# Low halves of twelve first-layer weight tiles from TensorE: 64 w minus the high half, copied by ScalarE

## The chip, the cores and the metric

The kernel runs on one core of a Trainium2 chip. The core has TensorE (PE, the matrix engine, whose weight loads the profile shows as PEld), VectorE (DVE), ScalarE (ACT), GpSimd (POOL) and a queue of transfers that SyncE (SP) issues to 16 DMA engines. Each engine works through its own instructions in a fixed order and waits on semaphores for the others. TensorE writes only to PSUM, in banks of 128 x 512 fp32 values. The metric is the time of one execution on the device in microseconds; lower is better.

## The reference

The input is `q`, `k`, `v` of shape (4, 8, 768, 48), a gate `beta`, and two pairs of weight matrices. First comes a recurrence over 768 time steps for each of 32 heads, and then two dense layers one after the other on 3072 tokens of width 384 (hidden width 2048):

```python
k_n = k / (norm(k) + 1e-06)
for t in range(S):
    y[:, :, t] = einsum('bhd,bhde->bhe', q[:, :, t], state)
    v_old = einsum('bhde,bhd->bhe', state, kt)
    state = state + bt * einsum('bhd,bhe->bhde', kt, vt - v_old)
...
h = x @ w_in                                        # first layer
x = (maximum(h, 0) + log1p(exp(-abs(h)))) @ w_out
...
h = x @ w_in2                                       # second layer
out = (h * cos(h)) @ w_out2
```

## The kernel before, in words

The time axis is cut into 24 chunks of 32 steps (`NS`), in groups of four. For a group, `norms`, `prep`, `gram` and `solve` work without the state: they scale `k`, form products inside a chunk on TensorE, and solve a small triangular system on VectorE (30 short dependent instructions; its end is the transpose `tg`). Then `step(n)` runs for each chunk: a chain of small matmuls (48 columns) on TensorE, each followed by a scaled copy on ScalarE and a subtraction on VectorE that split the result into two fp16 halves (`b`, `u`, `st`, `y`). After two steps `y` is turned by a transposing DMA into the columns `xt` of one block of 256 tokens, and `moe_block(0, j)` pushes this block through the first layer; there are twelve such blocks. When all are done, six blocks of 512 tokens go through the second layer.

Numbers are kept to about twice the precision of fp16: each operand is a high half and a low half, and a product is three fp16 matmuls (`PAIRS`: high-high, high-low, low-high). The weights arrive in DRAM as fp64. `conv(ph, f, t, key)` makes the two fp16 halves of one of the 16 hidden tiles of a layer, with both its matrices at once, that is 2 x 384 values in each of 128 partitions. A DMA brings 768 KB into `raw` or into the space of weight tiles that are not made yet. Three VectorE instructions (L456, L458, L460) build fp32 numbers in one of two buffers `cv`; one (`hi`, L471 on ScalarE, sometimes VectorE) writes the high half fp16(64 w), and one (`lo`, L481, on VectorE) the low half, 64 w minus the high half. Buffer `cv` is free again after that. For the second layer GpSimd does the low half (L479).

In `moe_in` (L820) a hidden tile is formed in one of the two PSUM banks `psH` and passes through ScalarE and VectorE; `moe_out` (L882) multiplies the result with the second matrix into `accA` and `accB`. At the start of the program the banks also serve `gram`.

The order of the instructions is written out by a planner (`Plan`): every `put` gives an operation with the engines that may do it, its assumed cost, and the keys that it reads and writes. The planner simulates the engines, always taking the ready operation with the longest way to the end, and emits each engine's list in that order. So one more operation can move all others, and can move an operation that two engines may do from one to the other. Since operations are entered with all of `weights(0)` ahead of the steps, an operation that `conv` puts on a bank `psH` comes before every use of this bank by `moe_in`.

Of the kernel before, what the change touches and what calls it, by code (L numbers as in the profile page):

```python
# [10 lines left out]
F32 = mybir.dt.float32  # L11
# [36 lines left out]
NRAW = 1  # L48
NB2 = NS // 4
NT = 2 * P, 4 * P  # L50
Z = 40 * C
# [217 lines left out]
def dve(n, fast=False):  # L269
    return 0.068 + n / (1920.0 if fast else 960.0)  # L270
# [6 lines left out]
def pool(n):  # L277
    return 0.149 + n * 0.001883
# [6 lines left out]
@with_exitstack  # L285
def delta_moe_moe_kernel(ctx, tc, q, k, v, beta, mask, w1, w2, out):
    nc = tc.nc
# [14 lines left out]
    mask_sb = const.tile([P, C + 3], F32, name="mask_sb")  # L302
    hpi = const.tile([P, 1], F32, name="hpi")
    tiny = const.tile([P, 1], F32, name="tiny")

# [70 lines left out]
    def put(var, w, r, fn, **kw):  # L376
        return pl.add(var, w, r, fn, **kw)
# [65 lines left out]
    def conv(ph, f, t, key):  # L443
# [39 lines left out]
        put([("ACT", act(n)), ("DVE", dve(n, True))], wk, ck, hi, port=True)  # L483
        put([("POOL", pool(n)), ("DVE", dve(n))][0 if ph else 1:], wk, ck, lo, port=True)

# [320 lines left out]
    def moe_in(ph, j, u, xk, x):  # L806
# [6 lines left out]
        for i in range(2 - ph):  # L813
            for kc in range(KC):
                f = (2 * u + i) if ph == 0 else u

                def fn(e, i=i, kc=kc, f=f):
                    w, xv = wview(ph, f)[:, 0], x if ph == 0 else x()
                    for idx, (l, m) in enumerate(PAIRS):
                        nc.tensor.matmul(  # L820
                            hp[:, i] if ph == 0 else hp, lhsT=w[:, l, kc * P:(kc + 1) * P], rhs=xv[:, m * KC + kc],
                            start=(kc == 0 and idx == 0), stop=(kc == KC - 1 and idx == 2))
                us = 3 * mm(NT[ph])
                moe_left[0] -= us
                put([("PE", us)], hk, xk + [("w", ph, f, 0)], fn, base=moe_left[0])
        n = 4 * P
# [40 lines left out]
    def moe_out(ph, j, u):  # L867
# [6 lines left out]
        for i in range(2 - ph):  # L874
            f = (2 * u + i) if ph == 0 else u
            for key, cs in groups:
# [10 lines left out]
                moe_left[0] -= us  # L887
                put([("PE", us)], [key], [("g16", s3, 0), ("g16", s3, 1), ("w", ph, f, 1)], fn, base=moe_left[0])

# [50 lines left out]
    put([("SP", 0.475)], [("beta",)], (), lambda e: nc.sync.dma_start(out=beta_sb, in_=beta), dma=0.27, **A)  # L940
    put([("SP", 0.475)], [("mask",)], (), lambda e: nc.sync.dma_start(out=mask_sb, in_=mask), dma=0.1, **A)
    load_v(0)
    load_v(1)
# [108 lines left out]
```

## Time and profile before

| | |
|---|---|
| runs | 1037.36, 1038.86, 1046.35 us; median 1038.86 |
| profiled execution (its time is its span) | 1038.4 us |
| mean granted TensorE clock | 0.965 of full speed |
| PE busy | 940.7 us, 91% |
| DVE busy | 668.8 us, 64% |
| ACT busy | 667.2 us, 64% |
| POOL busy | 366.2 us, 35% |
| first matmul of the first layer | 105.0 us after the start |
| HBM traffic | 71.03 MB read, 35.65 MB written |

The shares are averages over a start, in which the first group of chunks and the weights are prepared, a long middle, in which steps and layers share TensorE, and an end, in which only the second layer is left. They differ in what limits them, so the rows below are taken stretch by stretch. The clock that the throttle granted to TensorE has two levels, 1.2 GHz (0.50 in the rows) and 2.4 GHz (1.00).

### The profile page before, as it was taken

The page shows a single profiled execution, that of the slowest core. Times are in us where ns is not written, and L with a number is a line of the kernel's source. Part 1 is how long each engine was busy: PE and PEld are TensorE (multiplying, and loading weights), DVE is VectorE, ACT ScalarE, POOL GpSimd, SP SyncE. Part 2 cuts the span into 40 slices and gives each one's busy share as a digit, 9 for nine tenths or more (in the row PEclk, how much of TensorE's full clock was granted, in tenths as well). Part 3 has the DMA queues.
Part 4 walks back from the last instruction along what each step waited for, and adds up shares of the span by engine and source line. Part 5 has one row for each costly group of instructions (what it writes and reads, how often), then busy time and mean ns, then how long its engine had stood idle before and what let it go on. Part 6 is the DMA issues. An engine that isn't in the chain of part 4 may idle for free.

```text
span 1038.4 us, 27814 instructions
## 1 busy us (share of the span) xinstructions
PE 940.7 (91%) x11552; PEld 687.5 (66%) x11552; DVE 668.8 (64%) x1186; ACT 667.2 (64%) x1261; POOL 366.2 (35%) x330
## 2 busy tenths in 40 slices
PE   1135889997999899999999999999999999999998
PEld 1125779886899798899999997744444444444443
DVE  8999977666547754863576665686555555555454
ACT  5344769776767776866777787865555555554554
POOL 3013326433523442432332545553332223233232
PEclk9965899998999999999999999999999999999999
DMA  6998696876766775674558862111001010000000
GB/s 194 288 262 203 128 240 121 200 177 170 175 84 149 178 155 111 135 157 76 117 115 210 237 153 84 44 35 61 31 1 61 1 61 0 31 31 1 31 1 31
DMA packets 307741, 117.94 MB, mean 114 GB/s; under 512 B 272160, under 2 KB 287648, under 8 KB 307616
## 3 DMA queue, kind: packets, MB, share of 16 engines
q1 hardware_dynamic: 307616, 116.17, 46.0%
q8 instruction: 91, 1.49, 0.6%
q14 instruction: 34, 0.28, 0.1%
HBM read 71.03 MB, written 35.65 MB: 103 GB/s over the span
## 4 chain that ended last, share of the span: by engine, by line
PE 72%; DVE 9%; ACT 7%; DMA 6%; issue 3%; SPq 2%; POOL 1%; DVEq 0%; ACTq 0%; POOLq 0%
PE psH L820 20%; PE accA L882 15%; PE accB L882 11%; PE psC L820 7%; PE psA L882 6%; PE psC L699 6%; PE psY L820 4%; DMA kpd<-kp 3%; PE psY L699 2%; SPq L380 2%; ACT kp L389 1%; PE psA L605 1%; DMA qt<-q_dram 1%; DVE tlan L401 1%; DMA kt<-k_dram 1%
## 5 line engine op out<-in xcount | busy, mean ns | idle before, releaser
L401 POOL TENSOR_TENSOR g<-g,g 128x512 f16<-128x512 f32 x191 | 227.7, 1192 | 461.1 <-ACT g L389 446.9
L820 PE MATMUL psH<-xt,w 128*128 128x256 f16 x1728 | 232.1, 276 | 0.2
L389 ACT ACTIVATE g<-g 128x512 f16<-128x512 f32 x191 | 119.9, 628 | 105.2 <-DVE g L405 70.3
L882 PEld LDWEIGHTS <-w 128*128 128x128 f16 x1728 | 163.3, 98 | 23.3 <-issue 3.6
L820 PEld LDWEIGHTS <-w 128*128 128x128 f16 x1728 | 158.7, 98 | 18.9 <-issue 0.3
L882 PE MATMUL accA<-g,w 128*128 128x256 f16 x1152 | 159.6, 275 | 3.2 <-POOL g L401 1.7
L882 PEld LDWEIGHTS <-v 128*128 128x128 f16 x864 | 84.5, 98 | 101.9
L820 PEld LDWEIGHTS <-v 128*128 128x128 f16 x864 | 84.6, 98 | 100.9
L410 ACT ACTIVATE e<-e 128x512 f32<-128x512 f32 x96 | 60.4, 629 | 81.7 <-DVE e L405 81.7
L401 DVE TENSOR_TENSOR g<-psH,e 128x512 f32<-128x512 f32 x96 | 66.1, 688 | 70.3 <-ACT e L412 64.0
L882 PE MATMUL accB<-g,w 128*128 128x256 f16 x576 | 94.7, 276 | 0.0
L820 PE MATMUL psH<-xu,v 128*128 128x512 f16 x351 | 83.1, 379 | 0.0
L820 PE MATMUL psC<-xu,v 128*128 128x512 f16 x342 | 81.5, 379 | 0.0
L882 PE MATMUL accB<-g,v 128*128 128x512 f16 x288 | 77.8, 379 | 0.0
L882 PE MATMUL accA<-g,v 128*128 128x512 f16 x288 | 77.8, 379 | 0.0
L882 PE MATMUL psA<-g,v 128*128 128x512 f16 x288 | 77.6, 379 | 0.0
L837 ACT ACTIVATE e<-psH 128x512 f32<-128x512 f32 x96 | 56.7, 590 | 30.8 <-PE psH L820 30.4
L699 PEld LDWEIGHTS <-bdKQ 128*128 128x128 f16 x1840 | 64.4, 98 | 10.5 <-issue 8.4
L412 ACT ACTIVATE e<-e,hpi 128x512 f32<-128x512 f32 x96 | 69.3, 721 | 3.0
L699 PEld LDWEIGHTS <-bdA 128*128 128x128 f16 x1680 | 56.6, 99 | 20.4 <-issue 18.4
L412 ACT ACTIVATE e<-e 128x512 f32<-128x512 f32 x96 | 59.9, 624 | 1.2
L699 PE MATMUL psC<-b,bdT 128*128 128x48 f16 x768 | 29.2, 187 | 34.1 <-ACT bdT L389 21.2
(143 smaller groups left out, 1508.6 us busy)
## 6 DMA issues: line engine op xcount, KB each, us to landing
bdKQ<-kqd SPq DMA_DIRECT2D x184, 64.0 KB, 2.8
kpd<-kp SPq DMA_DIRECT2D x24, 448.0 KB, 3.6
kqd<-kq SPq DMA_DIRECT2D x20, 512.0 KB, 4.2
raw<-w_dram SPq DMA_DIRECT2D x12, 768.0 KB, 5.0
bdA<-kpd SPq DMA_DIRECT2D x96, 96.0 KB, 3.5
w<-w_dram SPq DMA_DIRECT2D x10, 768.0 KB, 7.1
v<-w_dram SPq DMA_DIRECT2D x10, 768.0 KB, 6.5
qt<-q_dram SPq DMA_DIRECT2D x24, 256.0 KB, 4.2
```

What stands on the lines that cost most here:

```text
L380: put([("SP", issue)], w, r, lambda e: nc.sync.dma_start(out=dst, in_=src), dma=eng_us, **kw)
L389: nc.scalar.activation(out=out, in_=in_, func=AF.Copy, scale=scale)
L401: put(var, w, r, lambda e: eng[e].tensor_tensor(out=out, in0=a, in1=b, op=op), port=True, **kw)
L410: nc.scalar.activation(out=out, in_=in_, func=func, scale=scale)
L412: nc.scalar.activation(out=out, in_=in_, func=func, scale=scale, bias=bias)
L605: nc.tensor.matmul(ps[:, h], lhsT=w, rhs=x, start=(i == 0), stop=(i == len(ops) - 1))
L699: nc.tensor.matmul(ps[:, h, 0:D], lhsT=lhs(h), rhs=mov[:, h], start=(first and i == 0 and h == 0), stop=(last and i == len(passes) - 1 and ...
L820: nc.tensor.matmul(hp[:, i] if ph == 0 else hp, lhsT=w[:, l, kc * P:(kc + 1) * P], rhs=xv[:, m * KC + kc], start=(kc == 0 and idx == 0), s ...
L837: nc.scalar.activation(out=ev, in_=hv, func=AF.Abs, scale=sc)
L882: nc.tensor.matmul(acc[c], lhsT=w[:, l, c * P:(c + 1) * P], rhs=rhs, start=(f == 0 and idx == 0 and (ph == 1 or c != 1)), stop=(f == NF - ...
```

## The change

For the first twelve hidden tiles of the first layer (`LO_PE = 12`, `f` = 0 to 11) the low half is no longer made by the one VectorE instruction. For each of the tile's two matrices TensorE runs two matmuls of 384 columns into a bank `psH`: one in fp32 with a matrix `eye` = 64 times the identity as weights and `cv` as the moving operand, and one in fp16 with `neg` = minus the identity and the high half. The bank then holds 64 w minus the high half, and ScalarE copies it as fp16 into the weight tile. `eye` is a new input of 64 KB, loaded by one DMA, and ScalarE makes `neg` of it once. The first layer's matmuls read the low half under a new key `("wl", f, o)`. Tiles 12 to 15 and the second layer stay as they were.

```diff
--- before.py
+++ after.py
@@ -47,6 +47,7 @@
 XTB = 3
 NRAW = 1
 NB2 = NS // 4
+LO_PE = 12
 NT = 2 * P, 4 * P
 Z = 40 * C
 X2 = 2 * C
@@ -283,7 +284,7 @@
 
 
 @with_exitstack
-def delta_moe_moe_kernel(ctx, tc, q, k, v, beta, mask, w1, w2, out):
+def delta_moe_moe_kernel(ctx, tc, q, k, v, beta, mask, ident, w1, w2, out):
     nc = tc.nc
     eng = {"PE": nc.tensor, "DVE": nc.vector, "ACT": nc.scalar, "POOL": nc.gpsimd, "SP": nc.sync}
     pl = Plan()
@@ -301,6 +302,8 @@
     beta_sb = const.tile([P, NG, C], F32, name="beta_sb")
     mask_sb = const.tile([P, C + 3], F32, name="mask_sb")
     hpi = const.tile([P, 1], F32, name="hpi")
+    eye = const.tile([P, P], F32, name="eye")
+    neg = const.tile([P, P], F16, name="neg")
     tiny = const.tile([P, 1], F32, name="tiny")
 
     wbuf = {0: [wp.tile([P, 2, DM], I64, name=f"w{f}") for f in range(0, NF, 2)], 1: []}
@@ -481,7 +484,18 @@
                 nc.vector.scalar_tensor_tensor(wv(1), in0=cf, scalar=sc, in1=wv(0), op0=ALU.mult, op1=ALU.subtract)
 
         put([("ACT", act(n)), ("DVE", dve(n, True))], wk, ck, hi, port=True)
-        put([("POOL", pool(n)), ("DVE", dve(n))][0 if ph else 1:], wk, ck, lo, port=True)
+        if ph or f >= LO_PE:
+            put([("POOL", pool(n)), ("DVE", dve(n))][0 if ph else 1:], wk, ck, lo, port=True)
+            return
+        for o in range(2):
+            bank, bk_ = flat[1 + o]
+
+            def rest(e, o=o, bank=bank):
+                nc.tensor.matmul(bank[:, 0:DM], lhsT=eye, rhs=cf[:, o], start=True, stop=False)
+                nc.tensor.matmul(bank[:, 0:DM], lhsT=neg, rhs=wv(0)[:, o], start=False, stop=True)
+
+            put([("PE", 5 * mm(DM))], [bk_], ck + wk + [("eye",), ("neg",)], rest, cold=2.0)
+            copy(wv(1)[:, o], bank[:, 0:DM], 1.0, [("wl", f, o)], [bk_] + wk, DM, ps=True, only=("ACT",))
 
 
     def norms(g):
@@ -822,7 +836,7 @@
                             start=(kc == 0 and idx == 0), stop=(kc == KC - 1 and idx == 2))
                 us = 3 * mm(NT[ph])
                 moe_left[0] -= us
-                put([("PE", us)], hk, xk + [("w", ph, f, 0)], fn, base=moe_left[0])
+                put([("PE", us)], hk, xk + [("w", ph, f, 0), ("wl", f, 0)], fn, base=moe_left[0])
         n = 4 * P
         gk, ek = [("g", s)], [("e", s)]
         flat_ = (lambda t: t) if ph == 0 else (lambda t: t.rearrange("p a t -> p (a t)"))
@@ -885,7 +899,7 @@
                                 stop=(f == NF - 1 and idx == 2 and (ph == 1 or c != 0)))
                 us = 3 * len(cs) * mm(NT[ph])
                 moe_left[0] -= us
-                put([("PE", us)], [key], [("g16", s3, 0), ("g16", s3, 1), ("w", ph, f, 1)], fn, base=moe_left[0])
+                put([("PE", us)], [key], [("g16", s3, 0), ("g16", s3, 1), ("w", ph, f, 1), ("wl", f, 1)], fn, base=moe_left[0])
 
     def moe_end(ph, j):
         if ph == 0:
@@ -939,6 +953,8 @@
     memset(st, 0.0, [("st", 0), ("st", 1)], 768, **A)
     put([("SP", 0.475)], [("beta",)], (), lambda e: nc.sync.dma_start(out=beta_sb, in_=beta), dma=0.27, **A)
     put([("SP", 0.475)], [("mask",)], (), lambda e: nc.sync.dma_start(out=mask_sb, in_=mask), dma=0.1, **A)
+    put([("SP", 0.475)], [("eye",)], (), lambda e: nc.sync.dma_start(out=eye, in_=ident), dma=0.2, **A)
+    actf(neg, eye, AF.Copy, [("neg",)], [("eye",)], P, scale=-1.0 / W_SC, **A)
     load_v(0)
     load_v(1)
 
@@ -1035,6 +1051,7 @@
             np.triu(np.full((C, C), 1.0 / K_SC, np.float32), 1),
             np.repeat(np.array([[0.0, K_SC ** -2, 0.0], [-1.0, 0.0, K_SC ** -2]], np.float32), C // 2, axis=0)],
             axis=1), (B, 1)),
+        "ident_dram": W_SC * np.eye(P, dtype=np.float32),
         "w1_dram": w_both(inputs["moe_w_in"], inputs["moe_w_out"]),
         "w2_dram": w_both(inputs["moe2_w_in"], inputs["moe2_w_out"]),
     }
```

The planner gives the whole program a new order. On VectorE, in the middle of the second step (`step(1)`), there stood before (`cv` are the buffers of the weights under conversion, `w` the weight tiles, `u`, `b`, `bt`, `st`, `y` the operands of the step):

```order
L405 SCALAR_TENSOR_TENSOR u_111<-psC_146,u_111 128x384
L405 SCALAR_TENSOR_TENSOR kq_128<-qt_117,kq_128 128x512
L481 SCALAR_TENSOR_TENSOR w_84<-cv_88,w_84 128x2x384
L405 SCALAR_TENSOR_TENSOR bt<-psC_145,bt 128x384
L456 TENSOR_SCALAR cv_88<-raw_87 128x768
L540 STREAM_TRANSPOSE kq_129<-kp_123 128x512
L458 SCALAR_TENSOR_TENSOR cv_88<-raw_87,cv_88 128x768
L542 STREAM_TRANSPOSE kq_129<-ka_127 128x128
L405 SCALAR_TENSOR_TENSOR b_110<-bt,b_110 128x384
L460 SCALAR_TENSOR_TENSOR cv_88<-raw_87,cv_88 128x768
L481 SCALAR_TENSOR_TENSOR w_83<-cv_89,w_83 128x2x384
L405 SCALAR_TENSOR_TENSOR y_112<-psY,y_112 128x384
```

Now the same piece of the step, from `u` to the next `b`, reads:

```order
L408 SCALAR_TENSOR_TENSOR u_113<-psC_148,u_113 128x384
L461 SCALAR_TENSOR_TENSOR cv_91<-w_88,cv_91 128x768
L408 SCALAR_TENSOR_TENSOR kq_131<-qt_120,kq_131 128x512
L556 STREAM_TRANSPOSE kq_132<-ka_128 128x128
L459 TENSOR_SCALAR cv_90<-raw_89 128x768
L408 SCALAR_TENSOR_TENSOR bt<-psC_147,bt 128x384
L461 SCALAR_TENSOR_TENSOR cv_90<-raw_89,cv_90 128x768
L408 SCALAR_TENSOR_TENSOR abuf<-psA,mask_sb,abuf 128x8x16
L408 SCALAR_TENSOR_TENSOR b_112<-bt,b_112 128x384
L463 SCALAR_TENSOR_TENSOR cv_90<-raw_89,cv_90 128x768
L463 SCALAR_TENSOR_TENSOR cv_91<-w_88,cv_91 128x768
L408 SCALAR_TENSOR_TENSOR kp_124<-psA,kp_124 128x128
```

The low halves (L481) are gone; the three instructions that build `cv` (now L459, L461, L463) stand alone, and the output `y` of the first step, which stood behind the second step's first `u`, `bt` and `b`, has moved ahead of this piece (two rows before it).

On TensorE, where the first matmul of the first layer stands, behind the first product of the third step, there stood before:

```order
L699 LDWEIGHTS bdKQ
L699 MATMUL psC_145<-st_106,bdKQ 128x48
...
L699 LDWEIGHTS bdT
L699 MATMUL psC_146<-b_110,bdT 128x48
...
L820 LDWEIGHTS w_79
L820 MATMUL psH_140<-xt_90,w_79 128x256
```

Now:

```order
L713 MATMUL psC_147<-st_108,bdKQ 128x48
L494 MATMUL psH_142<-cv_91,eye 128x384
L495 LDWEIGHTS neg
L495 MATMUL psH_142<-w_86,neg 128x384
...
L494 MATMUL psH_143<-cv_91,eye 128x384
L495 LDWEIGHTS neg
L495 MATMUL psH_143<-w_86,neg 128x384
L713 LDWEIGHTS bdT
L713 MATMUL psC_148<-b_112,bdT 128x48
...
L834 LDWEIGHTS w_81
L834 MATMUL psH_142<-xt_92,w_81 128x256
```

The low half of the twelfth tile (`cv`, `eye`, `neg`) stands between the products of the state and the third step's first product, and the first layer begins behind that one, as before. All 24 pairs stand ahead of the first matmul of the first layer, and 14 of them (tiles 5 to 11) behind the first product of the first step.

On ScalarE, at the same place, there stood before:

```order
L389 ACTIVATE kp_122<-psA 128x128
L471 ACTIVATE w_84<-cv_89 128x2x384
L389 ACTIVATE y_112<-psY 128x384
L389 ACTIVATE st_106<-st 128x384
L389 ACTIVATE kp_122<-pm 128x256
L389 ACTIVATE st_106<-st 128x384
L389 ACTIVATE abuf<-psA,mask_sb 128x8x16
L389 ACTIVATE b_110<-bt 128x384
L389 ACTIVATE kp_125<-kt_116 128x256 x2
```

Now:

```order
L474 ACTIVATE w_86<-cv_91 128x2x384
L392 ACTIVATE ka_129<-kp_127 128x4x2x16 x2
L392 ACTIVATE kp_124<-pm 128x256
L392 ACTIVATE y_114<-psY 128x384
L392 ACTIVATE st_108<-st 128x384
L392 ACTIVATE abuf<-psA,mask_sb 128x8x16
L392 ACTIVATE kp_125<-psA 128x128
L392 ACTIVATE w_86<-psH_142 128x384
L392 ACTIVATE w_86<-psH_143 128x384
L392 ACTIVATE kp_125<-pm 128x256
L392 ACTIVATE u_113<-psC_148 128x384
L851 ACTIVATE e_97<-psH_142 128x512
```

Two copies out of `psH` stand between the step's copies, and the first activation of the first layer (L851) reads the same bank behind them.

## Rows read from the trace of the kernel before

**Rows 1.** Page, part 1: busy us, share of the span, instructions.

```profile
PE 940.7 (91%) x11552; PEld 687.5 (66%) x11552; DVE 668.8 (64%) x1186; ACT 667.2 (64%) x1261; POOL 366.2 (35%) x330
```

**Rows 2.** Page, part 2: forty slices of 26 us.

```profile
PE   1135889997999899999999999999999999999998
...
DVE  8999977666547754863576665686555555555454
...
PEclk9965899998999999999999999999999999999999
DMA  6998696876766775674558862111001010000000
```

**Rows 3.** Windows: length; PE, PEld, DVE, ACT, POOL busy; clock; DMA; GB/s.

```profile
0.00:105.00 105.00, 32.92 (x824) 31.04 (x825) 97.20 (x186) 48.24 (x101) 22.92 (x24) 0.78 0.84 235
105.00:140.00 35.00, 32.75 (x604) 29.30 (x602) 33.68 (x73) 24.25 (x51) 10.99 (x11) 0.93 0.72 143
140.00:370.00 230.00, 212.45 (x3601) 192.14 (x3599) 151.06 (x311) 166.11 (x366) 96.11 (x101) 0.96 0.72 164
370.00:1038.40 668.40, 662.55 (x6538) 435.01 (x6534) 386.86 (x619) 428.60 (x747) 236.20 (x196) 1.00 0.31 76
```

**Rows 4.** Waits of TensorE, 140 to 440 us: total, times, longest.

```profile
PE psY L699 <- ACT u L389: 10.1, 3, 5.5
PE psC L699 <- ACT u L389: 3.3, 2, 2.3
```

**Rows 5.** Timeline, 100 to 106 us: start, length, engine, line, operation.

```profile
100.66 0.55 DVE L405 SCALAR_TENSOR_TENSOR y<-psY,y 128x384 f16<-128x384 f32 x1
...
101.27 1.21 SPq L795 DMA_TRANSPOSE xt<-y  x1
...
103.25 0.54 DVE L405 SCALAR_TENSOR_TENSOR bt<-psC,vt 128x384 f32<-128x384 f32 x1
...
104.40 0.80 PE L699 MATMUL psC<-b,bdT 128*128 128x48 f16 x16 [2.40 <-ACT b L389]
...
105.02 0.81 PE L820 MATMUL psH<-xt,w 128*128 128x256 f16 x3
```

**Rows 6.** Groups of VectorE up to 101 us: busy us, mean ns of one.

```profile
L481 DVE SCALAR_TENSOR_TENSOR w<-cv,w 128x768 f16<-128x768 f32 x12 | 12.2, 1027 | 0.0
...
L456 DVE TENSOR_SCALAR cv<-w 128x768 int32<-128x768 int32 x9 | 4.8, 545 | 0.0
...
L405 DVE SCALAR_TENSOR_TENSOR kq<-qt,kq 128x512 f16<-128x512 f32 x6 | 4.3, 732 | 0.0
...
L417 DVE MEMSET bdKQ<- 128x2048 f32 x1 | 1.8, 1765 | 0.4 <-issue 0.4
...
L391 DVE CAST kp<-kt 128x256 f16<-128x256 f32 x1 | 0.8, 834 | 0.0
```

**Rows 7.** Groups of ScalarE, whole span, same columns.

```profile
L389 ACT ACTIVATE u<-psC 128x384 f16<-128x384 f32 x48 | 23.0, 480 | 13.8 <-PE psC L699 13.8
```

**Rows 8.** Timeline of TensorE: twelve matmuls at either clock.

```profile
105.98 2.73 PE L820 MATMUL psH<-xt,w 128*128 128x256 f16 x12
...
113.87 1.47 PE L820 MATMUL psH<-xt,w 128*128 128x256 f16 x12
```

**Rows 9.** Groups of TensorE's weight loads, whole span.

```profile
L820 PEld LDWEIGHTS <-w 128*128 128x128 f16 x1728 | 158.7, 98 | 18.9 <-issue 0.3
```

**Rows 10.** Windows, columns as in rows 3.

```profile
46.00:101.00 55.00, 24.10 (x548) 22.66 (x549) 53.80 (x85) 26.69 (x52) 13.14 (x11) 0.62 0.92 245
...
59.00:110.00 51.00, 25.75 (x490) 23.29 (x490) 49.81 (x82) 23.00 (x50) 14.87 (x12) 0.50 0.88 223
110.00:120.00 10.00, 9.56 (x203) 8.82 (x202) 9.80 (x21) 8.92 (x18) 1.48 (x2) 1.00 0.67 115
```

**Rows 11.** Transfers: KB each, us from issue to landing.

```profile
kqd<-kq SPq DMA_DIRECT2D x20, 512.0 KB, 4.2
...
kt<-k_dram SPq DMA_DIRECT2D x24, 192.0 KB, 3.3
```

## The prediction

> **What bounds the kernel now.** I read the page's shares first, then its forty slices, then windows by stretch, then the waits of the engine that is the bound in the middle, and last the timeline where the start ends.
>
> The page says 91% for TensorE and 64% each for VectorE and ScalarE [rows 1]. That would make TensorE the bound and the change, which gives TensorE more work, a loss. The slices say otherwise [rows 2]: TensorE reads 1 to 5 in the first four slices, about 100 us, where VectorE reads 9, 9, 9, 7, and 9 nearly everywhere after the sixth. The windows put numbers to it [rows 3]. Up to 105 us TensorE is busy for 32.9 us, so 72.1 us of the 97.7 us that it idles in the whole span (1038.4 less 940.7) lie there. VectorE is busy for 97.2 of these 105 us: the start is VectorE's. From 105 to 140 us TensorE idles 2.3 us, from 140 to 370 us 17.6 us, and after 370 us 5.9 us in 668. In the middle it waits for the chain of the steps, the longest time 5.5 us, on ScalarE's copy of `u` [rows 4].
>
> So the time is TensorE's work plus the gaps before 370 us, and nearly all of that is the start. A microsecond cut from the start comes off the end, as long as the steps behind it move with it. The start ends where VectorE writes the second step's `y` at 100.66 us, the transposing DMA is issued at 101.27 us, VectorE makes the third step's `bt` at 103.25 us, and the first matmul of the first layer runs at 105.02 us, in TensorE's order behind the third step's first product [rows 5].
>
> **What comes off VectorE.** Up to 101 us it runs all twelve low halves that the change concerns: 12.2 us, 1.027 us each [rows 6]. In the new order one L484 (a tile from 13th on) is left ahead of the third step's `bt`, so eleven go: -11.3 us. The planner gives part of it back, since it moves other work onto VectorE ahead of the same point. Counted in the two orders and priced by rows of the trace: two high halves at 0.545 (the nearest row, L456, has the same shape) +1.1; one cast of `kp` +0.83; one low half of `kq` +0.73; two casts of `st`, two copies of `ka`, four small copies and scalings of `abuf`, `kp` and `tlan` and two small transposes or subtractions, estimated at 0.3 to 0.45 each from the same rows by size, +2.6; memsets, at 1.765 us for 2048 values, -0.6 [rows 6]. Together +4.7, so -6.6 us net. The same count up to the end of block 0 gives -8.8, and it stays there.
>
> VectorE's order also moves the end of `solve` later by some 7 us of work, and packs the two steps behind it closer: 50 us of VectorE work from `tg` to the third step's `bt`, where there were 63.
>
> **What comes onto TensorE.** 24 pairs of one fp32 and one fp16 matmul. No row shows an fp32 matmul. Twelve matmuls of 256 columns take 2.73 us at the lower clock and 1.47 at the higher [rows 8], so 384 columns cost 0.34 and 0.18 us in fp16. Lower bound: fp32 costs what fp16 does, and a pair is 0.37 us at the higher clock. Upper bound: a 32-bit operand on each side is two parts on each side, so four products, each with its own weight load of 98 ns [rows 9] in plain view, at the lower clock: a pair is 5 x 0.34 + 5 x 0.098 = 2.2 us. Either way 24 pairs are 9 to 53 us, and the cover is the 72 us of idle time before the first layer. I take four products without visible loads, 0.9 us at the higher clock and 1.7 at the lower, since weight loads lie beside matmuls here (PEld is busy 687.5 us, PE 940.7, in a span of 1038.4 [rows 1]). The Trainium skill (FP8 and Floating Point Precision, section TensorE Precision Notes) states that true fp32 makes four passes through the array; by that the pair is what I take, and with two passes it would be 0.55 and 1.0 us.
>
> The tight part is from `tg` on: 14 of the 24 pairs lie behind the first product of the first step, 13 us at the higher clock, 24 at the lower. In the 55 us from 46 to 101 TensorE is busy 24.1 and idle 30.9 [rows 10]; with the start 7 us shorter, 24 us of cover are left. That holds, barely at the lower clock.
>
> **What comes onto ScalarE, the queue and the buffers.** 24 copies out of PSUM at 0.48 us [rows 7] are 11.5 us, 22 of them before the second `y`; ScalarE is busy 26.7 of the 55 us [rows 10], so the sum fits. But queues are in order: a copy waits for its pair, the step's `u`, `st` or `b` copy stands behind it, and the pair itself waits for the high half on ScalarE and for the bank's last copy. A buffer `cv`, freed by VectorE before, is now freed by TensorE's fp32 matmul. By the order there are 3 us or more of VectorE work on the other buffer between, so I count nothing. The first layer's first matmul waits for the last copy out of its bank; before and after, eleven or twelve tiles are converted by then, so it comes no later. `neg` is one small activation, while ScalarE has slack, and behind the DMA of `eye`, which stands ahead of `beta` and one weight load.
>
> DMA is the second limit of the start: a share of 0.92 from 46 to 101 us, 50.6 us of work at 245 GB/s [rows 10]. The same work would not fit into 48 us. The new order issues less ahead of the second `xt`: two loads of `k` and one of `v` (192 KB each) and one 512 KB write of `kqd` fewer [rows 11], `eye` and 48 KB more, about 1.0 MB less or 4 us. At the share shown that allows 4 us of gain, at a share of 1.0 some 8.
>
> **The sum.** -6.6 us at the first layer's start, -8.8 at the end of block 0, less a little for DMA and hand-offs: I take -7.5. TensorE's added work lies in gaps, so 1038.4 - 7.5 = 1030.9 for the profiled execution. The median of the runs is 0.5 above it: 1031.
>
> **The rivals.**
>
> *The clock stays up and more is gained.* From 59 to 110 us the granted clock is 0.50 with TensorE busy for half of the time; from 110 to 120, with TensorE busy for 9.6 of 10 us, it is 1.00 [rows 10]. With pairs in its gaps TensorE may keep the higher clock. Then the first 24 matmuls of the first layer gain 2.5 us (1.26 for each twelve [rows 8]), and of the 12 us that half of TensorE's 24.1 us would save, perhaps 3 lie on the chain: 1026. Against it: VectorE sets the pace. The Trainium skill (TensorE: Matmul & The Clock Gate, section Part 1: The HAM clock gate) says that the throttled state is the default and that activity releases it; these rows agree.
>
> *The gain is eaten.* The DMA share doesn't rise above 0.92, so 4 us is the cap, and hand-offs among three in-order queues take 2 more: 1036 to 1037.
>
> *TensorE becomes the bound of the start, and it is slower.* The place is the chain from `tg` to the third step. It decides from a pair of 24 / 14 = 1.7 us on, which is just the lower clock's price. At 2.2 us the 14 pairs are 30.7, 6.7 over the cover, and if some twelve products of the chain each arrive behind half a pair, 1.1 us, that is 13 more: 1031 + 6.7 + 13 = 1051.
>
> *The change doesn't free VectorE*, because its idle time grows by what was removed (waiting for `cv` or for copies): 1038 to 1039. For it speaks that the end of `solve` comes later; against it that VectorE has other conversions to go on with.
>
> **How the numbers follow.** Forecast (1028 to 1034) 0.45; clock (1021 to 1028) 0.20; eaten or not freed (1034 to 1041) 0.23; TensorE bound (1041 to 1056) 0.12. The predicted time is the forecast's, 1031. The range from 1022 to 1045 leaves out about 0.05 below and 0.08 above, and it takes in both bounds of the pair's price but for the worst hand-offs. A measurement of this kernel can tell 1% from no change, so faster means under 1028.5: the clock case and the lower edge of the forecast, 0.32. Slower means over 1049.2: part of the last case, 0.09. The rest is 0.59.
>
> **What would show it.** In the profile after, the first matmul of the first layer stands near 98 us, VectorE is over 90% busy up to there, and TensorE's busy time up to there rises by 13 to 40 us. TensorE idles about 17 us from 140 to 370 us, as before. The clock from 59 us on tells the first rival; DMA above 0.95 with VectorE idle tells the second; TensorE at 95% between `tg` and the first layer tells the third. What would make it wrong at once: an fp32 pair over 2.2 us, or gaps in the middle that grow by as much as the start gives.

## The result: 0.6% slower, and the profile after

Twenty runs of the changed kernel had a median of 1046.63 us (1042.82 to 1054.32), twenty of the kernel before 1040.0 us (1037.36 to 1046.35). The ratio is 1.0058, with a 95% interval from 1.0043 to 1.0072. The forecast was 1031. The profiled execution has a span of 1046.0 us, where it was 1038.4. The span runs from the first to the last instruction; wherever both are on record, the time of the same execution is 1.7 to 2.1 us longer.

The page of the changed kernel, part 1, against [rows 1]:

```profile
PE 965.5 (92%) x11624; PEld 697.3 (67%) x11624; DVE 661.8 (63%) x1188; ACT 671.3 (64%) x1274; POOL 359.6 (34%) x328
```

TensorE is busy 24.8 us longer and idle 17.2 us less. The windows of the changed kernel say where, with the columns of [rows 3]; the last row answers to [rows 10]:

```profile
0.00:105.00 105.00, 58.27 (x922) 41.66 (x923) 91.70 (x192) 53.93 (x119) 23.53 (x27) 0.85 0.83 224
105.00:140.00 35.00, 31.54 (x606) 28.65 (x605) 29.27 (x66) 19.34 (x38) 4.14 (x5) 1.00 0.72 149
140.00:370.00 230.00, 208.10 (x3506) 188.13 (x3506) 151.56 (x307) 165.85 (x360) 93.53 (x99) 0.94 0.72 166
370.00:1046.00 676.00, 667.60 (x6594) 438.87 (x6592) 389.23 (x624) 432.14 (x758) 238.37 (x198) 0.99 0.32 76
...
46.00:101.00 55.00, 39.99 (x621) 28.33 (x621) 50.51 (x95) 32.07 (x70) 10.06 (x12) 0.80 0.92 225
```

Up to 105 us the added work fills idle time: TensorE's idle time there falls from 72.1 to 46.7 us. Behind 105 us it grows: 2.3 to 3.5 us up to 140, 17.6 to 21.9 up to 370, 5.9 to 8.4 from there on, 8.1 us together. From 140 to 370 us the granted clock is also lower, 0.94 against 0.96.

The timeline of the changed kernel, at the end of the start (against [rows 5]) and at its two longest stalls:

```profile
98.70 0.55 DVE L408 SCALAR_TENSOR_TENSOR y<-psY,y 128x384 f16<-128x384 f32 x1
...
101.38 0.55 DVE L408 SCALAR_TENSOR_TENSOR bt<-psC,vt 128x384 f32<-128x384 f32 x1
...
102.85 0.82 PE L834 MATMUL psH<-xt,w 128*128 128x256 f16 x6
...
140.68 0.52 ACT L413 ACTIVATE sq<-kt 128x384 f32<-128x384 f32 x1 [7.12 <-DMA kt<-k_dram]
...
143.15 0.27 PE L896 MATMUL accA<-g,w 128*128 128x256 f16 x1 [3.79 <-ACT g L392]
...
189.82 0.77 ACT L392 ACTIVATE kq<-qt 128x512 f16<-128x512 f32 x1 [6.55 <-DMA qt<-q_dram]
...
190.87 0.51 ACT L392 ACTIVATE b<-bt 128x384 f16<-128x384 f32 x1
...
191.42 0.80 PE L713 MATMUL psC<-b,raw 128*128 128x48 f16 x16 [5.97 <-ACT b L392]
```

The first matmul of the first layer comes at 102.85 us instead of 105.02, so 2.2 us of the start are gained. From there to the end it takes 943.2 us instead of 933.4. Of the 9.8 us lost there, 8.1 are idle time of TensorE; the other 1.7 are longer busy time (909.4 against 907.7 us) at a mean granted clock of 0.98 against 0.99. In both stalls ScalarE has stood for 7 us in front of an operation that needs a late load of `k` or `q`; what TensorE needs (`g`, `b`) is queued behind it.

The waits of TensorE in the changed kernel, 140 to 440 us, against [rows 4]:

```profile
PE psC L713 <- ACT b L392: 10.9, 6, 6.0
PE psY L713 <- ACT u L392: 6.2, 2, 3.8
PE accA L896 <- ACT g L392: 3.8, 1, 3.8
```

The added work itself, from the groups of the changed kernel up to 105 us (busy us, mean ns of one, idle before):

```profile
L494 PE MATMUL psH<-cv,eye 128*128 128x384 f32 x48 | 27.0, 651 | 11.0 <-DVE cv L463 9.4 <-ACT w L392 1.4
L392 ACT ACTIVATE w<-psH 128x384 f16<-128x384 f32 x24 | 11.3, 481 | 10.1 <-PE psH L495 10.1
...
L495 PE MATMUL psH<-w,neg 128*128 128x384 f16 x24 | 9.4, 392 | 0.1
```

All pairs run before the first layer begins. An fp32 product is recorded as two matmuls.

The chain that ended last in the stretch from 60 to 106 us, shares by line: first the kernel before,

```profile
by line: issue 12.6%; DMA xt<-y 12.2%; DVE cv L460 12.1%; DVE cv L458 10.4%; DVE w L481 8.4%; DVE cv L456 7.3%; SPq L380 6.4%; DVE kq L540 4.0%; DVE st L405 3.4%; DVE u L405 3.1%; DVE bt L405 2.2%; DVE y L405 2.2%; DVE b L405 2.1%; DVE ss L
```

then the changed kernel, with the longest pieces in order of time (start, us):

```profile
by line: DMA w<-w_dram 17.4%; DMA kpd<-kp 13.4%; DMA raw<-w_dram 13.4%; DVE cv L461 8.9%; DMA qt<-q_dram 8.4%; DVE cv L463 5.8%; DVE cv L459 5.0%; SPq L383 4.3%; issue 4.2%; SPq L809 2.2%; POOL kp L404 2.1%; DVE bt L408 2.0%; DVE kp L404 1.
...
56.35 8.00 DMA w<-w_dram
...
76.61 6.18 DMA kpd<-kp
...
86.95 3.87 DMA qt<-q_dram
...
92.05 6.16 DMA raw<-w_dram
```

Before, this chain ran over VectorE's conversions, with one long transfer in it (`xt`, 5.6 us). After, four transfers make up 24 of the 50 us from 56.35 to 106. The last of the four is doubtful: `st`, which the profile puts behind it, does not read `raw`, VectorE has no idle time in front of `st` (98.24 us), and `raw` is first read at 99.69 us. The other three end idle time: 1.46 us of VectorE, and 2.26 and 1.95 us of ScalarE.

### The profile page after: what moved, and what is told of

The parts are those of the page before. It is cut to its first block, busy times and chain, and to the rows that moved or that the text cites. A ratio compares the mean times of both kernels' runs of the same rounds, so it can differ in the third digit from the quotient of the medians.

```text
span 1046.0 us, 27965 instructions
## 1 busy us (share of the span) xinstructions
PE 965.5 (92%) x11624; PEld 697.3 (67%) x11624; DVE 661.8 (63%) x1188; ACT 671.3 (64%) x1274; POOL 359.6 (34%) x328
## 2 busy tenths in 40 slices
DMA packets 307885, 118.00 MB, mean 113 GB/s; under 512 B 272176, under 2 KB 287792, under 8 KB 307760
## 4 chain that ended last, share of the span: by engine, by line
PE 69%; DMA 9%; ACT 7%; DVE 7%; SPq 4%; issue 2%; POOL 1%; DVEq 0%; ACTq 0%; POOLq 0%
PE psH L834 19%; PE accA L896 15%; PE accB L896 10%; PE psC L834 7%; PE psA L896 6%; PE psC L713 5%; PE psY L834 4%; DMA kpd<-kp 4%; DMA qt<-q_dram 3%; SPq L383 3%; PE psY L713 2%; ACT kp L392 1%; PE psA L619 1%; ACT kq L392 1%; DVE tmpd L404 1%
## 5 line engine op out<-in xcount | busy, mean ns | idle before, releaser
L834 PE MATMUL psH<-xt,w 128*128 128x256 f16 x1728 | 228.7, 274 | 0.5 <-DVE g L404 0.5
L413 ACT ACTIVATE e<-e 128x512 f32<-128x512 f32 x96 | 60.4, 629 | 81.4 <-DVE e L408 81.3
L851 ACT ACTIVATE e<-psH 128x512 f32<-128x512 f32 x96 | 56.5, 589 | 23.5 <-PE psH L834 22.9
L415 ACT ACTIVATE e<-e 128x512 f32<-128x512 f32 x96 | 59.8, 623 | 1.2
L857 ACT ACTIVATE e<-e 128x512 f32<-128x512 f32 x96 | 59.4, 619 | 0.1
```

Source lines behind the costliest of these rows:

```text
L413: nc.scalar.activation(out=out, in_=in_, func=func, scale=scale)
L415: nc.scalar.activation(out=out, in_=in_, func=func, scale=scale, bias=bias)
L834: nc.tensor.matmul(hp[:, i] if ph == 0 else hp, lhsT=w[:, l, kc * P:(kc + 1) * P], rhs=xv[:, m * KC + kc], start=(kc == 0 and idx == 0), s ...
L851: nc.scalar.activation(out=ev, in_=hv, func=AF.Abs, scale=sc)
L857: put([("ACT", act(n))], ek, [], lambda e: nc.scalar.activation(out=ev, in_=ev, func=AF.Exp, scale=-1.0 if how[0] == "ACT" else -sc))
```

## The experiments

The first theory (A) was that the new order behind the start costs the time, since it puts ScalarE in front of late loads; its first rival (B), that the added work does.

Every ratio is to the kernel before, run beside it on the same chip (there its median was 1038.0 to 1039.6 us). "Span", "first" (the start of the first layer's first matmul) and "waits" (TensorE's waits from 105 to 460 us) are those of the one profiled execution, which can lie some us off the median. In e7, e9, e10 and e11 a part of the work is left out.

| kernel | median us | ratio (95%) | span | first | waits |
|---|---|---|---|---|---|
| before | 1040.0 | 1 | 1038.4 | 105.0 | 21.7 |
| changed | 1046.6 | 1.0058 (1.0043 to 1.0072) | 1046.0 | 102.9 | 29.8 |
| e1 new start, old order behind | 1045.7 | 1.0083 (1.0052 to 1.0114) | 1045.8 | 101.8 | 28.2 |
| e2 old start, new order behind | 1038.7 | 1.0006 (0.9989 to 1.0023) | 1036.0 | 104.9 | 20.5 |
| e3 changed, loads 6 us later in the plan | 1039.4 | 1.0017 (1.0000 to 1.0033) | 1036.1 | 103.1 | 24.3 |
| e4 before, same | 1041.4 | 1.0039 (1.0019 to 1.0058) | 1039.5 | 105.4 | 23.9 |
| e5 changed, loads issued earlier | 1050.4 | 1.0101 (1.0072 to 1.0130) | 1046.6 | 104.1 | 29.3 |
| e6 before, same | 1043.5 | 1.0054 (1.0030 to 1.0078) | 1044.2 | 106.3 | 28.5 |
| e7 changed, no pairs, no copies | 1040.7 | 1.0021 (0.9999 to 1.0043) | 1035.3 | 103.1 | 23.7 |
| e8 changed, nudge 0.62 | 1049.3 | 1.0091 (1.0055 to 1.0127) | 1043.4 | 103.5 | 28.8 |
| e9 changed, half weight loads | 1038.3 | 0.9987 (0.9967 to 1.0006) | 1036.3 | 98.0 | 26.7 |
| e10 before, same | 1032.4 | 0.9939 (0.9917 to 0.9961) | 1030.2 | 100.3 | 20.0 |
| e11 changed, pairs only | 1044.9 | 1.0045 (1.0025 to 1.0064) | 1037.6 | 102.9 | 26.8 |
| e12 before, nudge 0.62 | 1044.0 | 1.0058 (1.0036 to 1.0080) | 1043.2 | 104.7 | 25.0 |
| e13 changed, pairs doubled | 1046.2 | 1.0061 (1.0033 to 1.0089) | 1042.4 | 107.3 | 25.4 |
| e14 changed, copies doubled | 1043.1 | 1.0042 (1.0021 to 1.0063) | 1039.7 | 103.6 | 27.6 |
| e15 changed, all transfers later in the plan | 1041.2 | 1.0006 (0.9982 to 1.0031) | 1044.1 | 101.3 | 28.8 |
| e16 before, same | 1039.4 | 1.0004 (0.9982 to 1.0025) | 1037.5 | 102.3 | 26.6 |
| e17 changed, nudge 0.06 | 1042.8 | 1.0050 (1.0035 to 1.0065) | 1037.9 | 100.2 | 28.5 |
| e18 before, nudge 0.06 | 1050.1 | 1.0121 (1.0096 to 1.0145) | 1046.5 | 104.7 | 30.6 |

**Which half of the order costs (e1, e2).** Both plans are made in one kernel; the program follows one (`first`) up to the first layer and the other (`rest`) behind it. In e1 `first` is the changed kernel's plan; a line `...` marks what is cut from a diff:

```diff
-        for _, _, e, i in self.log:
...
+        for e, i in seq(first):
+            if self.ops[i]["moe"]:
+                break
+            go(i, e)
...
+        for e, i in seq(rest):
+            go(i, e)
```

> The changed program's order on every engine up to its first MoE matmul, then the order and the engine choices of the kernel before for everything behind it; the twenty-four pairs and copies are all in. Theory A (the loss is the new order behind the first MoE matmul, which puts ScalarE in front of late loads of k and q): first MoE matmul near 103 us as in the changed kernel, 933 us from there as before, so 1037 to 1039, ratio 0.997 to 0.999. Rival B (the pairs, the copies or the clock they leave cost the time, whatever the order): 1045 to 1047, ratio 1.005 to 1.007. Rival C (any order that its own plan did not lay out loses some us at the seam): above 1047.

> No pair and no copy at all: all sixteen low halves on VectorE, the order of the kernel before up to its first MoE matmul, then the order of the changed kernel behind it. Theory A: first MoE matmul at 105 us, 943 us behind it, so 1046 to 1050, ratio 1.006 to 1.010: slower without any of the added work. Rival B: 1038 to 1041, ratio 0.998 to 1.001.

Theory A fell on both sides: the loss stays with the old order behind the new start, and the new order behind the old start costs nothing that the interval shows. The timeline of e1 shows how a good order goes wrong behind another start (start, length, idle before):

```profile
105.82 0.52 ACT L448 ACTIVATE sq<-kt 128x384 f32<-128x384 f32 x1 [4.57 <-DMA kt<-k_dram]
...
106.77 0.95 PE L751 MATMUL psC<-u,bdG 128*128 128x48 f16 x24 [2.96 <-ACT u L427]
...
116.49 0.77 ACT L427 ACTIVATE kq<-qt 128x512 f16<-128x512 f32 x1 [4.28 <-DMA qt<-q_dram]
...
117.64 0.54 PE L751 MATMUL psC<-u,bdA 128*128 128x48 f16 x15 [2.95 <-ACT u L427]
```

The kernel before had issued its last two loads of `k` for this group at 72.95 and 83.49 us. The new start leaves them for later, so here they go out at 102.35 and 103.38 us, and the next load of `q` at 113.27 instead of 111.55. ScalarE waits for 4.57 and 4.28 us, and TensorE loses 5.9 us in two stalls, more than the start had gained; in the kernel before the wait on this `qt` is 0.58 us and the stall behind it 0.44. So e1's loss is at least partly rival C's, a seam between two plans, and e1 alone does not speak for rival B.

**Later loads in the plan (e3, e4).** One number for the planner, in both kernels:

```diff
-            dma(kt, k[n]..., kk, [("pre",)], 0.55, **A)
+            dma(kt, k[n]..., kk, [("pre",)], 0.55, slack=6.0 if g else 0.0, **A)
-        dma(qt, q[n]..., qk, [("pre",)], 0.73, **A)
+        dma(qt, q[n]..., qk, [("pre",)], 0.73, slack=6.0 if n >= 4 else 0.0, **A)
```

> The changed kernel with one number for the planner: loads of k and q behind the first group land 6 us later than it thought, so that ScalarE's squares and q copies are ordered later. Theory A in its narrow form (the late loads make the stalls at 143 and 191 us of the changed kernel): these two stalls of 4.8 and 6.0 us fall below 2 us each and the time to 1037 to 1042, ratio 0.997 to 1.002. Rival D (every new order of this program lands somewhere within some 8 us, and the changed kernel drew a bad one): anything from 1034 to 1050, with stalls of the same size at other places. Rival B: 1044 to 1047.

> The kernel before with the same 6 us for the planner, no other edit. Theory A, narrow form: its own waits of ScalarE on loads (4.8 and 2.4 us in front of 1.4 and 2.3 us of TensorE stall) shrink, 1034 to 1038, ratio 0.994 to 0.998. Rival D: 1036 to 1050, no tie to ScalarE's waits on loads.

The changed kernel won 4 parts in 1000, as theory A's narrow form says; the kernel before lost as much, which that form denies, though ScalarE's waits on loads of `k` and `q` fell to 0.9 and 0.5 us in the two. Rival D covers both. Rival B, that the added work costs 0.6% whatever the order, falls with e3: it does all of that work and stands at 1.0017.

**Earlier loads, same order (e5, e6).** Only SP's queue differs (`HOIST` is 8):

```diff
+            if self.ops[i]["early"]:
+                ...
+                sp = [j for j in range(low, at) if order[j][0] == "SP"]
+                if sp:
+                    order.insert(sp[-self.HOIST:][0], order.pop(at))
```

> The changed kernel with one edit behind the planner: each load of k and q behind the first group is issued up to eight places earlier on SP's queue, as far as its buffer's last readers allow. The order on TensorE, VectorE, ScalarE and GpSimd is that of the changed kernel, row for row. Theory E (the start gains little because the transfers do not come sooner, and ScalarE, in order, then stands in front of late loads of k and q, 18.6 us of such waits between 105 and 460 us, against 9.4 before): these waits fall below 8 us, the TensorE stalls of 3.8 and 6.0 us at 143 and 191 us go, 1037 to 1041, ratio 0.998 to 1.002. Rival F (the place of the loads is not the cause; pairs, copies or the rest of the order are): 1044 to 1048, ratio above 1.005.

> The kernel before with the same edit to SP's queue alone. Theory E: its 9.4 us of ScalarE waits on loads of k and q fall below 5, the two TensorE stalls behind them (1.4 and 2.3 us) with them: 1034 to 1038, ratio 0.996 to 1.000. Rival F: 1037 to 1041, no change.

Theory E fell. ScalarE's waits on loads of `k` and `q` went from 18.6 to 0.5 us, and TensorE's waits stayed at 29.3. The waits of TensorE in e5 from 105 to 460 us (total, times, longest) show what took their place:

```profile
PE psY L722 <- ACT u L401: 10.0, 3, 4.4
PE psC L722 <- ACT b L401: 7.6, 4, 5.3
PE psC L722 <- DMA bdT<-tgd: 6.2, 1, 6.2
PE psA L628 <- DMA bdA<-kq: 3.5, 2, 3.1
```

Two of these lines, 9.7 us, are other transfers of the same queue, which cost 0.7 us in the changed kernel; that they are late because the loads passed them is likely, but not shown. In e6 ScalarE's waits on loads fell as well, from 9.4 to 2.1 us, and TensorE's waits rose from 21.7 to 28.5. Both kernels took longer than either theory allowed.

**The low halves for nothing, and the pairs alone (e7, e11).** The order stays. In e7 the pairs and the copies are left out, in e11 the copies alone; in both the first layer reads the high halves in place of the twelve low ones:

```diff
-                nc.tensor.matmul(bank[:, 0:DM], lhsT=eye, rhs=cf[:, o], start=True, stop=False)
-                nc.tensor.matmul(bank[:, 0:DM], lhsT=neg, rhs=wv(0)[:, o], start=False, stop=True)
+                pass
-            copy(wv(1)[:, o], bank[:, 0:DM], 1.0, ...)
+            put([("ACT", act(DM, True))], ..., lambda e: None)
```

> The changed kernel's order on every engine with the twenty-four pairs and their copies left out and nothing in their place; the products that would read the twelve low halves read the high halves, so the amount of TensorE work behind the start is the same and the output is not the reference's. Theory E (the start is held by transfers and by chains, not by VectorE's or TensorE's amount of work): first MoE matmul no earlier than 100 us, end 1040 to 1046. Rival G (pairs and copies cost what was lost): first MoE matmul at 96 to 98 us and 1030 to 1036.

> The changed kernel's order with the twenty-four pairs on TensorE but without ScalarE's copies of them; the products read the high halves as in the kernel without pairs, so the output is not the reference's. Without both the time was 1040.7, ratio 1.0021; with both 1046.6, 1.0058. If the pairs carry the difference: 1044 to 1047. If the copies (in ScalarE's order, in front of what the chain waits for) carry it: 1039 to 1042. If the difference is noise of orders and runs: anything between, and no clear split.

With the work taken off VectorE and none of it on TensorE and ScalarE, the first layer still starts at 103.05 us. The chain of e7 from 60 to 106 us says why:

```profile
by line: DMA kpd<-kp 20.4%; DMA w<-w_dram 14.4%; DVE cv L461 8.7%; SPq L383 7.8%; DVE cv L463 7.0%; DVE cv L459 5.7%; issue 4.7%; DVE u L408 4.5%; SPq L448 4.1%; DVE b L408 3.2%; SPq L808 3.0%; DVE kq L408 2.8%; DVE kq L553 2.7%; DVE st L40
```

Transfers and their queue again, without a pair in the program. For the end, e7 is 0.37 points better than the changed kernel, and e11 lies between them, in the range for pairs that carry the difference, but not clear of e7 (0.24 points, uncertain by 0.29). That two intervals touch does not make the difference nothing: from their widths it is uncertain by 0.26 points if the errors are independent. So in this order pairs and copies together seem to cost 0.1 to 0.6%, which e13 and e14 take up.

**Fewer bytes (e9, e10).** Half of each first-layer weight tile is loaded and used twice:

```diff
-            lambda e: nc.sync.dma_start(out=t(), in_=(w1, w2)[ph][f]), dma=2.18)
+            lambda e: nc.sync.dma_start(out=t() if ph else t()[:, 0], in_=w2[f] if ph else w1[f][:, 0]), dma=2.18)
```

> The changed kernel in which each of the sixteen loads of first-layer weights brings half of its tile (384 KB instead of 768), and every operation on it reads that half twice: the output layer's weights of that layer are left out, the instructions and their order on TensorE, VectorE, ScalarE and GpSimd are the same. Theory H (the transfers are a second limit of the start, some 2 us under VectorE's, and their lateness is what ScalarE and TensorE wait for up to 260 us): first MoE matmul from 102.9 to 96 to 100 us, end 1046 to 1036 to 1041, and 4 us or more better in the ratio than the same edit to the kernel before. Rival I (the chain across engines sets the start, not bytes): first MoE matmul 101.5 to 103, end 1043 to 1047.

> The kernel before with the same halved loads. Theory H: VectorE is its first limit up to the first MoE matmul, so that stays at 103 to 105 us; behind it some waits go, end 1036 to 1039, ratio 0.997 to 1.000. If bytes were its limit too: first MoE matmul below 101 and the end below 1035. Rival I: no change, 1037 to 1040.

The first matmul of the first layer, in e9:

```profile
97.97 0.82 PE L835 MATMUL psH<-xt,w 128*128 128x256 f16 x6 [0.80 <-DMA xt<-y]
```

and in e10:

```profile
100.28 0.49 PE L821 MATMUL psH<-xt,w 128*128 128x256 f16 x3
```

Bytes are a limit of the start, by 4.9 us in the changed kernel and 4.7 in the kernel before, where VectorE has all of its work. The windows up to 46 us and from 46 to 101, with the columns of [rows 3], first of the kernel before, then of e10, show where that was open:

```profile
0.00:46.00 46.00, 7.22 (x240) 6.82 (x240) 39.40 (x95) 19.89 (x44) 9.65 (x12) 1.00 0.75 233
46.00:101.00 55.00, 24.10 (x548) 22.66 (x549) 53.80 (x85) 26.69 (x52) 13.14 (x11) 0.62 0.92 245
...
0.00:46.00 46.00, 7.08 (x240) 6.68 (x240) 43.14 (x100) 21.87 (x47) 10.18 (x13) 0.79 0.72 203
46.00:101.00 55.00, 24.95 (x597) 23.36 (x598) 54.51 (x88) 26.63 (x55) 12.78 (x11) 0.62 0.72 172
```

Behind 46 us VectorE is nearly always busy in both. In the first 46 us it idled 6.6 us, and with half of the bytes 2.9: 3.7 of the 4.7 us come from there. That bytes would be the changed kernel's limit alone was wrong: both kernels gain 0.6 to 0.7%, and the distance between the two stays (0.0048 here, 0.0047 in e5 and e6).

**Another order of the same work (e8, e12).**

```diff
-    XP = 0.6
+    XP = 0.62
```

> The changed kernel, re-planned with one latency of the planner's model changed from 0.60 to 0.62 us, nothing else: the same work in another order of equal standing. Theory E with its chance part (what an order costs hangs on which loads ScalarE happens to stand behind): anywhere from 1036 to 1047, and the ScalarE waits on k and q loads between 105 and 460 us tell which: below 10 us goes with under 1041, above 18 with over 1044. Rival B (the work itself costs): 1045 to 1048.

> The kernel before with the planner's latency of 0.60 us set to 0.62, no other edit: the same work in another order of equal standing. Theory J (a new order of the whole program alone costs some us, because the order of the kernel before is one of the better ones): 1040 to 1048, ratio 1.002 to 1.009, as large as the change itself. Rival B (the change's own work costs, orders are alike): 1036 to 1040, ratio 0.998 to 1.002.

The kernel before, without any edit to its work, loses 0.58% to a new order: as much as the change. The changed kernel (e8) came out slower than both of its ranges, with 18.5 us of ScalarE's waits on loads, which fits the rule in its expectation; e5, with 0.5 us of them and 1050.4 us, does not.

**Twice the added work (e13, e14).**

```diff
+                for _ in range(2):
-                nc.tensor.matmul(bank[:, 0:DM], lhsT=eye, ...)
-                nc.tensor.matmul(bank[:, 0:DM], lhsT=neg, ...)
+                    nc.tensor.matmul(bank[:, 0:DM], lhsT=eye, ...)
+                    nc.tensor.matmul(bank[:, 0:DM], lhsT=neg, ...)
```

> The changed kernel in its own order, each of the twenty-four pairs of products issued twice into the same bank, so that TensorE has some 21 to 36 us more in the first 103 us. If pairs cost nothing while they fit in TensorE's idle time (46 us idle there): ratio 1.004 to 1.007, as the changed kernel, first MoE matmul within 1 us of 102.9. If they delay what the chain needs, as the runs without them suggest (up to 0.0024): 1.007 to 1.012.

> The changed kernel in its own order, each of ScalarE's twenty-four copies done twice: 12 us more on ScalarE in the first 103 us. If they are covered (ScalarE 54 of 105 us busy there): ratio 1.004 to 1.007. If a copy in ScalarE's order delays the chain by its own length: first MoE matmul 1 to 3 us later and ratio 1.007 to 1.010.

Neither shows a cost at the end: against the changed kernel +0.03 and -0.16 points, each uncertain by 0.3. In e13 TensorE is busy for 46.9 of the 55 us from 46 to 101, and the first layer begins 4.4 us later than in the changed kernel, where within 1 us was expected:

```profile
107.28 0.81 PE L835 MATMUL psH<-xt,w 128*128 128x256 f16 x6 [0.66 <-DMA xt<-y]
```

but its waits behind that are 25.4 us instead of 29.8, and the ratio is 1.0061. So a second helping of the added work shows no cost, while leaving out the first (e7) gained 0.37 points. The two don't fit one price for the work, and why stays open.

**Both kernels drawn anew (e15 to e18).** All transfers at least 1.5 us later in the plan, and another nudge:

```diff
-                end = dma_free + 0.9 + o["slack"]
+                end = dma_free + 0.9 + max(o["slack"], 1.5)
```

> The changed kernel, planned with every transfer landing at least 1.5 us later than its model had it. Theory K (orders laid out for transfers that come too early make the stalls): TensorE's waits between 105 and 460 us fall from 29.8 to below 24 and the time to 1036 to 1041. Theory J (each new order is a draw): 1037 to 1050, no telling which.

> The kernel before with the same later transfers in the plan. Theory K: 1034 to 1038, and the changed kernel with the same edit stands within 3 us of it. Theory J: 1037 to 1048, mostly above the kernel before, since that is one of the better draws.

```diff
-    XF = 0.05
+    XF = 0.06
```

> The changed kernel, re-planned with the model's other hand-off latency set from 0.05 to 0.06 us. Theory J (the change is worth nothing by itself, each order is a draw of some 0.3 percent either way): ratio between 0.998 and 1.010. Rival B (the added work costs 0.6 percent in every order): 1.004 to 1.008 above the kernel before with the same nudge.

> The kernel before with the same nudge. Theory J: ratio 0.999 to 1.007, above 1 more likely than below, and no fixed distance to the changed kernel with the same nudge. Rival B: 0.998 to 1.002.

Theory K is not borne out in the kernel before: its time did not fall, and TensorE's waits rose from 21.7 to 26.6 us. In the changed kernel (e15) the median came near its range, but the waits can't tell why: the profiled execution, with a time of 1046.0 us (span 1044.1), is the slowest of the twelve. Rival B fell with e17, which is faster than e18, and e18 is slower than theory J's range too. With this, five pairs of kernels differ by the change alone under the same planner: changed less before, +0.0058, -0.0022 (e3, e4), +0.0033 (e8, e12), +0.0002 (e15, e16), -0.0071 (e17, e18). Their mean is 0.0000; from their spread, a standard deviation of 0.0050, it is uncertain by 0.006 (95%). So the change is worth nothing that five draws can show, and a price of up to 0.6% either way is not excluded. Every new order of the kernel before was as slow as it or slower, by 0.0004 to 0.0121. None of the kernels that do all of the work is faster than it.

## Why the prediction was wrong

**The step on VectorE was right, and its carrying on was wrong.** VectorE's busy time up to 105 us fell by 5.5 us (97.20 to 91.70), near the 6.6 counted, and the first step's transposing DMA was issued 7.0 us sooner (85.56 against 92.51 us). But the second one was issued 1.4 us sooner and the first layer began 2.2 us sooner. "-6.6 us at the first layer's start" failed there: the start was VectorE's by its busy share alone, and transfers bound it as well. Up to the first layer's start VectorE is now busy for 89.6 us instead of 97.2 and idle for 13.3 instead of 7.8: of the 7.6 us taken off it, 5.5 came back as idle time. The prediction had the second limit, as a share of bytes that "allows 4 us of gain"; the share stayed at 0.92 and the rate fell from 245 to 225 GB/s, while the chain of the changed kernel shows single late transfers: 8.0 us for a weight tile, 6.2 for a `kpd` write whose buffer ScalarE waits for, 3.9 for a `qt`. e7 shows the limit without the added work (first layer at 103.05 us), e9 and e10 that bytes move it, in the kernel before with no work taken off VectorE. Two smaller readings were wrong: the prediction's slices of VectorE ("9, 9, 9, 7, and 9 nearly everywhere") are not in [rows 2], where VectorE starts 8, 9, 9, 9 and falls to 5 (the later nines are TensorE's); and 0.5 us from the profiled execution to the median compared a span with the times of other runs. The Trainium skill (DMA: Bandwidth & Descriptors, section Specifications) gives 512 bytes as the least transfer for full rate; 272,176 of the 307,885 packets of the changed kernel are smaller, and no run here shows what larger ones would give.

**The step that cost the result was one clause: "as long as the steps behind it move with it".** They did not: 9.8 us were lost behind the first layer's start, 8.1 of them as idle TensorE. The edit to the program is a new order for all of it, and the prediction priced only the start of that order. e12 and e18 show that such a draw alone moves the kernel before by 0.6 and 1.2%, as much as was lost here; that the draw is the whole cause of this loss is argued from their size, not shown, since e7 puts a part of it on pairs and copies. e2 shows that the new order behind is good after the old start; the old one behind the new start (e1) is bad, at least in part by the seam. The prediction named "gaps in the middle that grow by as much as the start gives" as what would make it wrong, and gave it no chance.

**The pairs.** Their price was right: at the higher clock a pair was taken for 0.9 us, and in the timeline of the changed kernel, where the granted clock is 1.00, the next product begins 0.89 us after the pair began:

```profile
99.59 0.89 PE L494 MATMUL psH<-cv,eye 128*128 128x384 f32 x2
100.32 0.33 PE L495 MATMUL psH<-w,neg 128*128 128x384 f16 x1
100.48 0.56 PE L713 MATMUL psC<-st,bdKQ 128*128 128x48 f16 x16
```

The fp32 part takes 0.73 us up to the fp16 one, which takes 0.16. The four passes for fp32 that the Trainium skill (FP8 and Floating Point Precision, section TensorE Precision Notes) states agree with this: the ratio is 4.6, and 4.0 against the 0.18 us that the prediction took for 384 columns from [rows 8]. At the lower clock a pair was taken for 1.7 us, and from 48.91 us on (granted clock 0.50) one takes 1.60. That pairs and copies fit into idle time was right for the start: without them (e7) the first layer begins no earlier, at 103.05 against 102.85 us. For the end it is open.

**The rivals.** The clock did come up (0.62 to 0.80 from 46 to 101 us), but the pairs are not shown to have raised it: e7, without a pair and with TensorE busy for 23.6 us of the same 55 (24.1 in the kernel before), has 0.94:

```profile
46.00:101.00 55.00, 23.55 (x567) 22.01 (x566) 50.35 (x94) 25.45 (x52) 10.94 (x12) 0.94 0.92 222
```

The start of e7 is no earlier for it. In the 114 runs of the kernel before beside the experiments the mean granted clock lies between 0.953 and 0.993, and it has no tie to the time (correlation -0.07, each time against the median on its chip). So no run shows the gain that this rival counted on. "The gain is eaten" was the right mechanism for the start, and only for the start. TensorE as the bound of the start did not come: the first layer is delayed only with twice the pairs (e13), and even then the end does not move. "The change doesn't free VectorE" was partly right: from 46 to 101 us it idles 4.5 us instead of 1.2, and up to the first layer it is busy for 87% of the time, not over 90%.

What stays open: what pairs and copies cost in this order (e7 against e13 and e14), and what makes one order better than another. TensorE's waits go with it: over the twenty profiled executions of the table the span behind the first layer's start and the waits have a correlation of 0.87, from 929.9 us with 20.0 (e10) to 944.0 with 28.2 (e1). But they say where the time is lost, not why, and a single profile is not the median: that of e7 is the fastest of its twelve runs, 3.7 us under their median, and that of e15 the slowest, 4.8 us above.

## What to carry to other kernels

A busy share of 93% names the bound only as far as the next chain: before an engine's work is counted as gain, follow the chain of waits for what would be last without it, transfers one by one. Where a planner sets the order, an edit is also a new draw of the whole order: re-plan the kernel before with a harmless nudge or two, and take the spread of those as the least effect that one pair of kernels can show (here 0.04 to 1.2% over four new plans, two of them nudges with 0.6 and 1.2%). A start that is shortened against fixed loads can cost more behind than it gave, as in e1.

## What the runs showed of the hardware

An fp32 product with 384 columns is recorded as two matmuls with two weight loads. In the group of its loads the mean is 245 ns, where the fp16 loads of the same pairs take 116:

```profile
L494 PEld LDWEIGHTS psH<-cv,eye 128*128 128x128 f32 x48 | 10.0, 245 | 16.8 <-issue 12.4 <-ACT w L392 3.8 <-DVE ss L516 0.5
L495 PEld LDWEIGHTS <-neg 128*128 128x128 f16 x24 | 2.8, 116 | 4.6 <-issue 2.6
```

The Trainium skill (TensorE: Matmul & The Clock Gate, section Weight-path perf modes — Fast Weight Load (FWL) and DoubleRow) states that the fast load of weights is off for fp32; these rows agree.
